# An attention and feed-forward kernel on one core: the first half of a weight loaded through another engine's queue, and a new order

## The chip, the cores and the metric

The kernel runs on one core of a Trainium2 chip. The metric is the device time of one execution in microseconds (us); lower is better. A core has five engines, each with its own instruction stream executed in order: PE (TensorE, matrix multiply; its weight loads are listed as PEld), DVE (VectorE), ACT (ScalarE), POOL (GpSimd) and SP (SyncE, which here only issues transfers). Transfers between the large memory and the core's own memory (DMAs) are issued by SP, ACT or POOL, each into a queue of its own, and are carried out by 16 DMA engines that all queues share.

## The reference

Inputs are q, k and v of 4 batches, 8 heads, 768 positions and 64 columns, a flag for each head, and three weights, all in float32.

```
scores = q @ k^T / 8
retrieval heads (flags 1 0 1 0 0 0 1 0): causal mask
the other heads: causal mask, and key among the first 4 or query - key < 64
a = softmax(scores);  attn = a @ v
x = attn, heads side by side: 3072 x 512
out = maximum(x @ w1, x @ w2) @ w_out      (512 -> 1024 -> 512)
```

## The kernel before, in words

The work is cut into eight halves: four batches (`b`), each in two halves of 384 queries (`hf`). Heads are taken in four pairs. Of (b, hf) = (0, 0), called half A, and (0, 1), called half B, the names appear in the list of first loads.

For a half, `prepare` casts q, k and v to bfloat16 (`cast`, `vcast`, on POOL, DVE or ACT), turns q and k on PE (`turn`, L756) and copies them out (`unturn`). `attend` computes scores (`S`, L945), exponentials on ACT (L964), masks on DVE (L983), weighted sums (`W`, L1008), and scales them into `x` (L1035). For batch 0, `x` is turned on PE (`TX`, L1128) and copied to `xt`.

The feed-forward part uses maximum(h1, h2) = relu(h1 - h2) + h2. So `prep_weights` makes w12 = w1 - w2 (`sub`, L1164, four quarters on DVE), casts w2 to bfloat16 (`w2b`), turns it on PE (`P`, L1180), copies it out (`w2t`) and multiplies it by w_out (`P2`, L1198) into `w2o`. `forward` then needs, for a half, eight up-projections of 4 matmuls with w12 (`F`, L1219), a relu each (L1243), and for each of three blocks of 128 rows 12 matmuls into one bank (L1269): 8 with w_out and 4 with `w2o`. Output is copied by `take_out` and stored at L1288.

**What sets the order.** No instruction is placed by hand. Each piece of work is an `Op` with a cost for each engine that may do it, the pieces that it depends on, and a rank. `Order.run` (L197) is a planner in Python that runs when the kernel is built: it keeps a clock, gives each engine as it comes free the ready piece of lowest rank, and emits the instructions in that order. Its times are guesses; on the chip each engine goes through its stream in the emitted order and waits on semaphores that follow from the data. The ranks (`RANK`, `FRONT`, `FRONT_STEP`, `STEP`, `FF_STEP`) and the margins are the result of a search. While PE has no ready work and the planner's clock is under 38 us (`WARM_UNTIL`), the planner puts in a matmul on a zero tile (`warmer`, L503).

**Loads.** `LOADS` (L405) lists the first loads: A and B are q and k of the two halves (L551, 768 KB each, rows of 768 bytes), Av and Bv their v in three pieces (L561, 256 KB each, rows of 256 bytes), w10, w11, w20, w21 the two halves of w1 and w2 (L637, 1 MB each, rows of 2 KB), wo0 to wo3 the quarters of w_out (L651, cast to bfloat16 on the way). All but w_out go through SP's queue. w_out goes through POOL's, and each quarter is first held back by a small copy (L650) that reads from an earlier load: which one follows from `PACE`: with 1 it is the last but one of the loads listed ahead of it (w_out itself not counted), with 2 the last but two. The staging memory has three slots: half A in the first, half B in the second, w2 in the third, and w1 in the first again, so w1 is loaded when half A's casts are done.

For queues the planner has a model: a load becomes active `DMA_LATE` after its issue, active queues share the rate by `grain` (its guess at a row's weight), and a queue takes no more loads when the `parts` of those in it exceed `RING`; SP then waits.

Of the kernel before, what the change touches and what calls it, by code (L numbers as in the profile page):

```python
# [15 lines left out]
ACT = mybir.ActivationFunctionType  # L16
# [98 lines left out]
class Op:  # L115
# [1 line left out]

    __slots__ = (
        "costs", "emit", "deps", "lat", "data", "end", "left", "users", "ready", "rank",
        "claims", "frees", "margin", "tag", "port", "bias", "share", "parts", "grain",  # L120
    )

    def __init__(self, costs, emit, deps=(), lat=0.13, data=None, rank=0.0, claims=(), frees=(),
                 margin=0.0, tag=None, port=(), bias=None, share=1.0, parts=1024, grain=18.0):
        self.costs, self.emit, self.lat, self.data, self.rank = costs, emit, lat, data, rank
        self.deps = [o for o in deps if o is not None]
        self.claims, self.frees, self.margin, self.tag = claims, frees, margin, tag
        self.port, self.bias, self.share, self.parts = port, bias or {}, share, parts
        self.grain = grain
        self.end, self.ready, self.users = None, 0.0, []  # L130


class Order:
# [63 lines left out]
    def run(self, names, allowed):  # L197
        free = dict.fromkeys(("PE", "ACT", "DVE", "POOL", "SP"), 0.0)
        free["SP"], free["PE"], free["POOL"] = 0.75, PE_BEGINS, MASKS_MADE - 0.45
        done_pe = []  # L200

        def used(t, span=3.4):
# [78 lines left out]
        while events:  # L281
            t = events[0][0]
            while events and events[0][0] <= t + 1e-9:
                _, _, o = heapq.heappop(events)
# [22 lines left out]
            while again:  # L307
# [22 lines left out]
                for relaxed in (False, True):  # L330
                    chosen = None
                    for n in ("S", *names) if last == "S" else names:
                        if at[n] >= len(self.lists.get(n, ())):
                            continue
                        o = self.lists[n][at[n]]
# [13 lines left out]
                    if chosen:  # L349
                        n, o = chosen  # L350
# [33 lines left out]
CAST_QK = {'POOL': 0.46, 'DVE': 0.27, 'ACT': 0.4}  # L384
CAST_V = {'POOL': 0.3, 'DVE': 0.26, 'ACT': 0.26}
RANK = {
    'cast': 1.75, 'vcast': 14.3, 'unturn': 1.4, 'mix_k': 0.0, 'mix_v': -21.35, 'exp': 1.0,
    'mask': -1.9, 'norm': -5.7, 'take_x': 2.25, 'turn': -5.95, 'w2b': 7.1, 'sub': -11.6, 'w2t':
    -11.15, 'wob': -4.75, 'w2o': -6.8, 'relu': -2.6, 'load': 7.35, 'out': -9.5, 'h2': 11.0,
    'table': -2.65, 'vload': 3.85,  # L390
}
NLD = 3
NQB = 4
# [43 lines left out]
ENTER_S = 0.1  # L437
# [7 lines left out]
FRONT = (  # L445
    {'mix_k': -29.1, 'mask': -2.4, 'unturn': -6.1, 'exp': -1.5, 'vcast': 3.3, 'cast': -24.7,
    'norm': -13.8}, {'vcast': 27.9, 'unturn': -12.7, 'exp': 5.4, 'mask': 33.1, 'norm': 9.1,
    'mix_k': 37.9, 'cast': -12.4},
)
FRONT_STEP = (30.1, 7.2)  # L450
UNTURN_BIAS = ({'ACT': 1.0}, {'ACT': 1.0})
SHARED = 0.89
UP_PARTS = 2


def tile_three_full_heads(
# [3 lines left out]
    nc = tc.nc  # L460
    B, H, S, D = q.shape
# [15 lines left out]
    w2b = keep.tile([128, KC, d_ff], BF16, name="w2b")  # L477
# [27 lines left out]
    order = Order(8, dummy, WARM_UNTIL)  # L505
    op, pe = order.op, order.pe
    eng = {"ACT": nc.scalar, "DVE": nc.vector, "POOL": nc.gpsimd}
    T = {}

    def copy(e, out, in_):  # L510
# [13 lines left out]
    def act(n):  # L524
        return 0.065 + n / 1200

    def dma(mb, emit, deps=(), rate=0.31, rank=0.0, old=None, parts=1024, grain=18.0):
        asked.append(rank)
        o = op({"SP": 0.5}, emit, deps, data=mb / rate, rank=rank + 1e-4 * len(asked), parts=parts, grain=grain)
        if old is not None:  # L530
            later.append((o, old))
        return o
# [11 lines left out]
    def load_half(b, hf, kinds=(0, 1, 2)):  # L544
# [11 lines left out]
            loads[b, hf, t].append(dma(mb, emit, old=old, rate=RATE["first"] if t == 0 and (b, hf) != (0, 0) else RATE["long"], grain=36.0))  # L556

        def piece(t, src, i):
            def emit(_):
                r0 = HALF * hf + 128 * i  # L560
                nc.sync.dma_start(  # L561
                    out=lds[:, s, t, :, i * D:i * D + D],
                    in_=src[b, :, r0:r0 + 128, :].rearrange("h p d -> p h d"),
                )
            loads[b, hf, t].append(dma(0.262, emit, old=old, rate=RATE["v"]))
# [62 lines left out]
    def load_up(name, src, c):  # L628

        if name not in T:  # L630
            s, staged_old[name], tenants[name] = slot()
            T[name] = lds[:, s].rearrange("p t h c -> p (t h c)")[:, 0:KC * d_ff] \
                .rearrange("p (c f) -> p c f", f=d_ff)
        n = d_ff // UP_PARTS

        def emit(_):
            nc.sync.dma_start(  # L637
                out=T[name][:, :, c * n:c * n + n],
                in_=src.rearrange("(c p) f -> p c f", p=128)[:, :, c * n:c * n + n],
            )  # L640
        return dma(
            2.097 / UP_PARTS, emit, old=staged_old[name], rate=RATE["w"] if UP_PARTS == 4 else RATE["w half"],
            parts=512, grain=180.0 / UP_PARTS,
        )

    def load_down(c, behind):

        def emit(_):
            for o in behind:
                nc.gpsimd.tensor_copy(out=landed, in_=place_of[o])  # L650
            nc.gpsimd.dma_start(  # L651
                out=wob[:, 2 * c:2 * c + 2],
                in_=wo.rearrange("(c p) f -> p c f", p=128)[:, 2 * c:2 * c + 2],
            )
# [1025 lines left out]
```

## Time and profile before

| | before |
|---|---|
| median of 3 runs (lowest to highest) | 182.91 us (182.77 to 182.97) |
| the profiled execution's own time | 183.0 us |
| its span, first to last instruction | 181.3 us |
| clock granted to TensorE | 0.998 |

The profiled execution has 1.7 us outside its span. A line of a timeline gives start and length in us, engine (a `q` behind it: its sequencer, which issues transfers and doesn't count as busy), line of the kernel, operation, output and inputs, and count; in brackets is how long the engine had been idle and what ended the wait. A line of the windows view gives a stretch, its length, the busy time and number of instructions of PE, PEld, DVE, ACT and POOL, TensorE's granted clock, the load of the DMA engines and the rate in GB/s. A line of issues ends with the KB of a transfer and the us from its issue to its landing. A line of a queue gives packets, MB and the share of the 16 engines.

### The profile page before, as it was taken

Reading aid. Unit: us, or ns where it says so; the run is one execution under the profiler, and the core shown is the slowest. Engines: PE = TensorE matmul, PEld = TensorE weight load, DVE = VectorE, ACT = ScalarE, POOL = GpSimd, SP = SyncE. Lnnn points to the kernel's source line nnn. Section 1 sums busy time; section 2 is a strip of 40 time slices with the busy share of each in tenths; the row PEclk is TensorE's granted clock in tenths of the full one; section 3 lists DMA queues with packets and bytes.
Section 4 is the critical chain, followed back from the end, with each engine's and each line's share of the span. In section 5 each row is a group of like instructions: output and inputs, shape, how many; then the busy total and the mean of one; then the engine's idle time right before and its main releaser. Section 6 shows DMA issues by size and latency. Waiting matters only on the chain.

```text
span 181.3 us, 4937 instructions
## 1 busy us (share of the span) xinstructions
PE 171.4 (95%) x1806; PEld 106.3 (59%) x1826; DVE 103.8 (57%) x301; ACT 130.9 (72%) x289; POOL 43.8 (24%) x88
## 2 busy tenths in 40 slices
PE   7999969999998999999999999999999999999992
PEld 7966836565655666556554764555466545545561
DVE  5688976798979997256666685944647500000000
ACT  3567965795999999999999895566798524525431
POOL 6524500100518049839665000000000000000000
PEclk9999999999999999999999999999999999999999
DMA  4999999999899999999999999930641052012013
GB/s 128 332 306 228 358 205 196 391 321 265 234 278 265 322 268 228 238 157 220 189 159 128 202 171 126 206 124 0 66 140 58 4 145 116 7 61 116 0 68 116
DMA packets 72529, 32.37 MB, mean 179 GB/s; under 512 B 53938, under 2 KB 67506, under 8 KB 72498
## 3 DMA queue, kind: packets, MB, share of 16 engines
q1 hardware_dynamic: 52448, 28.45, 64.8%
q0 software_dynamic: 19904, 3.41, 26.7%
q8 instruction: 16, 0.26, 0.6%
q10 hardware_dynamic: 146, 0.13, 0.2%
q14 instruction: 15, 0.12, 0.2%
HBM read 25.17 MB, written 6.29 MB: 174 GB/s over the span
## 4 chain that ended last, share of the span: by engine, by line
PE 66%; DMA 14%; DVE 6%; issue 4%; SPq 4%; POOL 1%; ACT 1%; DVEq 0%; POOLq 0%; ACTq 0%
PE ps L1269 32%; PE ps L1219 17%; PE ps L945 7%; PE ps L1008 5%; DMA ld<-in_k_dram 5%; DMA ld<-in_v_dram 5%; DMA wob<-in_moe_w_out_dram 5%; SPq L551 3%; PE ps L756 2%; DVE x L1035 2%; SPq L561 2%; PE ps L1198 1%; DVE at L983 1%; POOL qb L514 1%; ACT at L964 1%
## 5 line engine op out<-in xcount | busy, mean ns | idle before, releaser
L964 ACT ACTIVATE at<-ps 128x512 bf16<-128x512 f32 (+2 forms) x134 | 65.1, 577 | 10.0 <-PE ps L945 9.2
L1269 PE MATMUL ps<-wob,g 128*128 128x512 bf16 (+1 forms) x194 | 45.9, 370 | 0.5 <-issue 0.3
L1219 PE MATMUL ps<-xt,w 128*128 128x384 bf16 x256 | 45.9, 326 | 0.0
L1219 PEld LDWEIGHTS <-w 128*128 128x128 bf16 x256 | 23.7, 98 | 14.7
L983 DVE TENSOR_TENSOR at<-at,tab 128x1024 bf16<-128x1024 bf16 (+5 forms) x49 | 25.3, 529 | 10.0 <-ACT at L964 9.9
L1243 ACT ACTIVATE g<-ps 128x384 bf16<-128x384 f32 x51 | 25.2, 502 | 5.9 <-PE ps L1219 5.7
L1269 PEld LDWEIGHTS <-g 128*128 128x128 bf16 x200 | 18.2, 98 | 18.7 <-issue 0.2
L512 ACT COPY ot<-ps 128x512 f32<-128x512 f32 (+1 forms) x19 | 10.7, 566 | 20.6 <-PE ps L1269 20.5
L1269 PE MATMUL ps<-w2o,xt 128*128 128x512 bf16 (+1 forms) x91 | 24.3, 370 | 0.5
L1008 PEld LDWEIGHTS <-at 128*128 128x128 bf16 x477 | 19.6, 97 | 7.4 <-issue 0.8
L1035 DVE TENSOR_TENSOR x<-ps,rez 128x192 f32 x64 | 22.7, 355 | 1.5
L1008 PE MATMUL ps<-vb,at 128*128 128x65 bf16 x387 | 21.4, 193 | 0.2
L945 PE MATMUL ps<-qk 64*128 64x128 bf16 (+1 forms) x322 | 19.9, 230 | 0.3
L945 PEld LDWEIGHTS <-qk 64*128 64x128 bf16 x322 | 11.9, 94 | 10.4 <-issue 7.8
L514 POOL CAST qb<-ld 128x384 bf16 (+1 forms) x21 | 9.7, 494 | 27.1 <-DVE x L1035 12.3
L1269 PEld LDWEIGHTS <-xt 128*128 128x128 bf16 x100 | 9.2, 98 | 8.7
L503 PE MATMUL ps<-warmer 128*128 128x128 bf16 x137 | 12.7, 254 | 1.2 <-POOL warmer L1613 1.2
L756 PE MATMUL ps<-tab,qb 128*128 128x128 bf16 x144 | 12.0, 219 | 1.8 <-POOL qb L514 0.5
L512 ACT CAST qb<-ld 128x192 bf16 (+1 forms) x24 | 8.7, 412 | 5.2 <-DMA ld<-in_k_dram 2.1
L1025 DVE RECIPROCAL rez<-ps 128x6 f32<-128x6 f32 x32 | 5.2, 183 | 11.6 <-PE ps L1008 11.4
L503 PEld LDWEIGHTS <-warmer 128*128 128x128 bf16 x137 | 10.8, 117 | 1.4 <-POOL warmer L1613 1.2
L756 PEld LDWEIGHTS <-qb 128*128 128x128 bf16 x144 | 9.0, 98 | 4.1 <-POOL qb L514 1.1
(69 smaller groups left out, 168.7 us busy)
## 6 DMA issues: line engine op xcount, KB each, us to landing
out_dram<-ot SPq DMA_DIRECT2D x23, 256.0 KB, 3.2
ld<-in_q_dram SPq DMA_DIRECT2D x6, 768.0 KB, 7.4
ld<-in_k_dram SPq DMA_DIRECT2D x6, 768.0 KB, 7.6
ld<-in_v_dram SPq DMA_DIRECT2D x18, 256.0 KB, 8.2
ld<-in_moe_w_dram SPq DMA_DIRECT2D x4, 1024.0 KB, 8.3
wob<-in_moe_w_out_dram POOLq DMA_DIRECT2D x4, 256.0 KB, 9.2
ld<-in_q_dram POOLq DMA_DIRECT2D x8, 96.0 KB, 11.3
ld<-in_k_dram POOLq DMA_DIRECT2D x8, 96.0 KB, 10.9
```

What stands on the lines that cost most here:

```text
L503: nc.tensor.matmul(banks[e][:, 0:128], lhsT=warm, rhs=warm, start=True, stop=True)
L512: nc.scalar.copy(out=out, in_=in_)
L514: eng[e].tensor_copy(out=out, in_=in_)
L756: nc.tensor.transpose(to[:, i], qbs[:, T["qb", n, hf] % NQB, t, i].rearrange("p h d -> p (h d)"), ident)
L945: nc.tensor.matmul(to.rearrange("p (i c) -> p i c", c=128), lhsT=lhsT, rhs=q_of(n, i, m)[rows], start=bk not in under, stop=True, skip_gro ...
L964: nc.scalar.activation(out=at[:, bk, 0:w], in_=bank(("ps", b, hf, t), part=bk)[:, 0:w], func=ACT.Exp, scale=scale,)
L983: eng[e].tensor_tensor(out=at, in0=at, in1=tbl, op=ALU.mult)
L1008: nc.tensor.matmul(po[:, hh, i - NT * hf, :], lhsT=ats[:, T["at", b, hf, t] % NAT, bk, e * 128:(e + 1) * 128], rhs=rhs, start=first, stop= ...
L1035: nc.vector.tensor_tensor(out=xs[:, (2 * b + hf) % NX, :, bass.ds(heads[2 * p + hh], 1), :], in0=po[:, hh, :, 0:D].unsqueeze(2), in1=z[:, ...
L1219: nc.tensor.matmul(bank(key)[:, 0:HALF], lhsT=w[:, kc, fc * 128:(fc + 1) * 128], rhs=xts[:, (2 * b + hf) % NXT, :, kc, :], start=(kc == 0) ...
L1243: nc.scalar.activation(out=g, in_=ph, func=ACT.Relu)
L1269: nc.tensor.matmul(bank(key)[:, cols], lhsT=lhsT, rhs=(w2o if kind == "x" else wob)[:, c, cols], start=(e == 0), stop=(e == len(steps) - 1),)
```

## The change

The first half of w2 (`w20`) is issued by ACT and no longer by SP. In the planner it depends on a piece that ends at 11.0 us and has rank -9, so ACT takes it as the first thing after the planner's 11.0 us. The list of loads changes; so, with `PACE` 2, do the loads that hold back w_out: wo0, wo1 and wo2 wait for the first piece of Av (before: second piece, third, third), wo3 for the second piece (before: w20). SP's limit goes from 4224 to 3300 parts, which holds three loads of 1024; the planner's latency becomes shorter for a load that waited for its queue; the `grain` of w_out goes from 90 to 50 and a half weight counts 768 parts, not 512. All ranks, margins and steps have new values. The other new names (`V_QUEUES`, `queues` for v) are there but empty or unused.

```diff
@@ begin
+            idle[e] = free[e]
...
-                push(t + (DMA_FIRST if t < 1.0 else DMA_LATE[e]), (e, o))
+                o.late = DMA_FIRST if t < 1.0 else max(RING_LATE, DMA_LATE[e] - max(0.0, t - max(o.ready, idle[e])))
+                push(t + o.late, (e, o))
...
-LOADS = ('A', 'B', 'Av', 'wo0', 'w20', 'wo1', 'wo2', 'w10', 'wo3', 'w21', 'Bv', 'w11')
-BIAS = {'DVE': 0, 'ACT': 0}
+LOADS = ('A', 'B', 'Av', 'wo0', 'wo1', 'wo2', 'w20', 'wo3', 'w21', 'Bv', 'w10', 'w11')
+BIAS = {'DVE': 0, 'ACT': 2.5}
...
-PACE = 1
+PACE = 2
...
-RING = {'SP': 4224, 'POOL': 6200, 'ACT': 4224}
+RING_LATE = 1.0
+RING = {'SP': 3300, 'POOL': 6200, 'ACT': 4224}
...
-    'first': 0.33, 'long': 0.32, 'v': 0.235, 'w': 0.355, 'w half': 0.39, 'wo': 0.37, 'cast':
+    'first': 0.33, 'long': 0.32, 'v': 0.225, 'w': 0.35, 'w half': 0.385, 'wo': 0.34, 'cast':
...
-STEP = 3.0
-FF_STEP = -2.9
-S_AFTER = 3
+STEP = 3.9
+FF_STEP = -2.2
+S_AFTER = 0
...
-MARGIN = {'W': 1.2, 'S': 0.2, 'F': 0.1, 'TQ': 0}
-X_MARGIN = 2.5
+MARGIN = {'W': 1.2, 'S': 0.2, 'F': 2.0, 'TQ': 0.8}
+X_MARGIN = 0.4
...
+BY_ACT = {'w20': 11.0}
+V_QUEUES = ()
...
+        by_act = name[:2] + str(c) in BY_ACT
+
         def emit(_):
-            nc.sync.dma_start(
+            queues["ACT" if by_act else "SP"].dma_start(
                 out=T[name][:, :, c * n:c * n + n],
                 in_=src.rearrange("(c p) f -> p c f", p=128)[:, :, c * n:c * n + n],
             )
         return dma(
-            2.097 / UP_PARTS, emit, old=staged_old[name], rate=RATE["w"] if UP_PARTS == 4 else RATE["w half"],
-            parts=512, grain=180.0 / UP_PARTS,
+            2.097 / UP_PARTS, emit, [order.given(BY_ACT[name[:2] + str(c)])] if by_act else (),
+            old=staged_old[name], rate=RATE["w"] if UP_PARTS == 4 else RATE["w half"],
+            parts=1536 // UP_PARTS, grain=180.0 / UP_PARTS, rank=-9.0 if by_act else 0.0,
+            by="ACT" if by_act else "SP",
         )
...
-            {"POOL": 0.9}, emit, behind, data=2.097 / 4 / RATE["wo"], grain=90.0, rank=-9.0, tag=f"wo{c}", parts=256
+            {"POOL": 0.9}, emit, behind, data=2.097 / 4 / RATE["wo"], grain=50.0, rank=-9.0, tag=f"wo{c}", parts=256
```

The new values of `RANK`, `FRONT`, `FRONT_STEP` and `UNTURN_BIAS` are left out here: all entries differ, and they enter only the planner's choice of what goes first.

More of the change, by code (lines that the diff above doesn't have):

```diff
@@ L119 @@
         "costs", "emit", "deps", "lat", "data", "end", "left", "users", "ready", "rank",
-        "claims", "frees", "margin", "tag", "port", "bias", "share", "parts", "grain",
+        "claims", "frees", "margin", "tag", "port", "bias", "share", "parts", "grain", "late",
     )
@@ L128, in __init__ @@
         self.port, self.bias, self.share, self.parts = port, bias or {}, share, parts
-        self.grain = grain
+        self.grain, self.late = grain, 0.0
         self.end, self.ready, self.users = None, 0.0, []
@@ L199, in run @@
         free["SP"], free["PE"], free["POOL"] = 0.75, PE_BEGINS, MASKS_MADE - 0.45
+        idle = dict(free)
         done_pe = []
@@ L386 @@
 RANK = {
[L387 to L390, printed above, removed]
+    'cast': 2.7, 'vcast': 12.75, 'unturn': 5.55, 'mix_k': 3.0, 'mix_v': -18.6, 'exp': -8.75,
+    'mask': 4.2, 'norm': -3.5, 'take_x': 1.25, 'turn': -2.9, 'w2b': 14.85, 'sub': -8.6, 'w2t':
+    -11.45, 'wob': -9.75, 'w2o': -2.15, 'relu': -6.45, 'load': 10.6, 'out': -10.45, 'h2': 9.35,
+    'table': -1.45, 'vload': -4.5,
 }
@@ L442 @@
 SHARE = {'S': 0.45, 'W': 0.8}
-MARGIN = {'W': 1.2, 'S': 0.2, 'F': 0.1, 'TQ': 0}
-X_MARGIN = 2.5
+MARGIN = {'W': 1.2, 'S': 0.2, 'F': 2.0, 'TQ': 0.8}
+X_MARGIN = 0.4
 FRONT = (
-    {'mix_k': -29.1, 'mask': -2.4, 'unturn': -6.1, 'exp': -1.5, 'vcast': 3.3, 'cast': -24.7,
-    'norm': -13.8}, {'vcast': 27.9, 'unturn': -12.7, 'exp': 5.4, 'mask': 33.1, 'norm': 9.1,
-    'mix_k': 37.9, 'cast': -12.4},
-)
-FRONT_STEP = (30.1, 7.2)
-UNTURN_BIAS = ({'ACT': 1.0}, {'ACT': 1.0})
+    {'mix_k': -26.4, 'mask': 13.8, 'unturn': -23.8, 'exp': 21.4, 'vcast': 6.5, 'cast': -6.4,
+    'norm': -43.7}, {'vcast': 58.2, 'unturn': -26.7, 'exp': 18.4, 'mask': 11.8, 'norm': 25.8,
+    'mix_k': 40.7, 'cast': 6.4},
+)
+FRONT_STEP = (37.7, -3.3)
+UNTURN_BIAS = ({'ACT': 1.0}, {'ACT': 0.5})
 SHARED = 0.89
 UP_PARTS = 2
+BY_ACT = {'w20': 11.0}
+V_QUEUES = ()
 def tile_three_full_heads(
@@ L507, in tile_three_full_heads @@
     eng = {"ACT": nc.scalar, "DVE": nc.vector, "POOL": nc.gpsimd}
+    queues = {"SP": nc.sync, "ACT": nc.scalar, "POOL": nc.gpsimd}
     T = {}
@@ L525, in act, with dma @@
         return 0.065 + n / 1200
-    def dma(mb, emit, deps=(), rate=0.31, rank=0.0, old=None, parts=1024, grain=18.0):
+    def dma(mb, emit, deps=(), rate=0.31, rank=0.0, old=None, parts=1024, grain=18.0, by="SP"):
         asked.append(rank)
-        o = op({"SP": 0.5}, emit, deps, data=mb / rate, rank=rank + 1e-4 * len(asked), parts=parts, grain=grain)
+        o = op(
+            {by: {"SP": 0.5, "ACT": 0.4, "POOL": 0.9}[by]}, emit, deps, data=mb / rate, rank=rank + 1e-4 * len(asked),
+            parts=parts, grain=grain,
+        )
         if old is not None:
@@ L558, in piece @@
         def piece(t, src, i):
+            by = next((e for *at, e in V_QUEUES if t == 2 and at == [b, hf]), "SP")
             def emit(_):
                 r0 = HALF * hf + 128 * i
-                nc.sync.dma_start(
+                queues[by].dma_start(
                     out=lds[:, s, t, :, i * D:i * D + D],
@@ L564, in emit @@
                 )
-            loads[b, hf, t].append(dma(0.262, emit, old=old, rate=RATE["v"]))
+            loads[b, hf, t].append(dma(
+                0.262, emit, old=old, rate=RATE["v"], rank=0.0 if by == "SP" else RANK["vload"], by=by,
+            ))
         long = (b, hf) in LONG
```

1 line of the change is left out of this document (removed).

## The prediction

> **What bounds the kernel now.** I read the page first: its span, its busy line and its groups.
>
> ```profile
> span 181.3 us, 4937 instructions
> PE 171.4 (95%) x1806; PEld 106.3 (59%) x1826; DVE 103.8 (57%) x301; ACT 130.9 (72%) x289; POOL 43.8 (24%) x88
> ...
> L503 PE MATMUL ps<-warmer 128*128 128x128 bf16 x137 | 12.7, 254 | 1.2 <-POOL warmer L1613 1.2
> ```
>
> PE is busy for 171.4 of 181.3 us, but 12.7 us of that are matmuls on the zero tile `warmer`, the fillers that the planner puts in while PE has nothing to do. So some 158.7 us are real work, which the change leaves alone, and the time is that work plus the stretches in which PE fills or waits. The windows view says where these are.
>
> ```profile
> 16.00:25.10 9.10, 7.31 (x131) 5.32 (x128) 8.39 (x27) 7.66 (x20) 3.71 (x8) 1.00 1.04 296
> 25.10:38.60 13.50, 13.31 (x169) 8.56 (x173) 9.54 (x21) 9.35 (x21) 0.63 (x2) 1.00 1.09 290
> ...
> 46.20:70.00 23.80, 22.96 (x294) 15.09 (x298) 21.36 (x60) 23.27 (x50) 10.49 (x25) 1.00 1.09 281
> ...
> 46.20:178.00 131.80, 129.34 (x1271) 76.17 (x1285) 66.96 (x195) 99.15 (x215) 31.45 (x53) 1.00 0.91 150
> ```
>
> The columns are the length, then the busy time of PE, PEld, DVE, ACT and POOL. PE lacks 9.10 - 7.31 = 1.8 us before 25.1 and next to nothing from there on; over the 131.8 us to 178 it lacks 2.5 us. So the front alone has something to give. PE's timeline shows how the front ends:
>
> ```profile
> 17.86 1.29 PE L1008 MATMUL ps<-vb,at 128*128 128x65 bf16 x32
> ...
> 25.12 1.47 PE L1198 MATMUL ps<-wob,w2t 128*128 128x512 bf16 x5 [1.66 <-DMA wob<-in_moe_w_out_dram]
> 26.43 0.67 PE L503 MATMUL ps<-warmer 128*128 128x128 bf16 x9
> ...
> 27.79 0.62 PE L1128 MATMUL ps<-tab,x 128*128 128x128 bf16 x8
> ...
> 38.03 2.76 PE L1219 MATMUL ps<-xt,w 128*128 128x384 bf16 x16
> ```
>
> At 25.12 PE had waited 1.66 us for the first quarter of w_out, without which the product w2 by w_out (L1198, `P2` in the planner) can't begin. At 38.03 the up-projection (L1219, `F`) begins, which needs w1. By then nearly all that PE can do without w1 is done. From 38 on work is plentiful: F and the output matmuls fill whatever attention leaves. **The end moves, to a first approximation, as the start of F at 38.03 moves.** Three things must come together for it: w1 landed, its difference with w2 made (L1164, on DVE), and PE's earlier work done. Here is the transfer side, SP's timeline and five of its landings:
>
> ```profile
> 3.65 2.19 SPq L551 DMA_DIRECT2D ld<-in_k_dram  x1
> 5.89 6.95 SPq L561 DMA_DIRECT2D ld<-in_v_dram  x3
> 12.88 2.96 SPq L637 DMA_DIRECT2D ld<-in_moe_w_dram  x2
> 15.88 10.88 SPq L561 DMA_DIRECT2D ld<-in_v_dram  x3
> 27.01 3.27 SPq L637 DMA_DIRECT2D ld<-in_moe_w_dram  x1
> ```
>
> ```profile
> ld<-in_k_dram SPq DMA_DIRECT2D x1, 768.0 KB, 9.6
> ...
> ld<-in_v_dram SPq DMA_DIRECT2D x1, 256.0 KB, 8.5
> ...
> ld<-in_v_dram SPq DMA_DIRECT2D x1, 256.0 KB, 6.7
> ...
> wob<-in_moe_w_out_dram POOLq DMA_DIRECT2D x1, 256.0 KB, 8.3
> ...
> ld<-in_moe_w_dram SPq DMA_DIRECT2D x1, 1024.0 KB, 8.3
> ```
>
> The order on SP is q, k of half A, q, k of half B, v of A in three pieces, both halves of w2, v of B, both halves of w1. Issues of 2.2 and 2.3 us each (B's k, each piece of v) are SP waiting for room in its queue. The landings are those of B's k (issued at 3.65, landed at 13.2), of the first piece of A's v (5.89, 14.4) and its last (after two issues of 2.3 us, at 10.6; 17.3), of the first quarter of w_out (16.76, 25.1, on POOL's queue) and of the first half of w1 (27.01, 35.3).
>
> **The change part by part.** *Both halves of w2 leave SP in one piece of 2.96 us; the first goes to ACT.* What ACT pays for one issue:
>
> ```profile
> 0.92 0.52 ACTq L1528 DMA_DIRECT2D raw<-in_is_retrieval_dram  x1
> ...
> 10.84 0.35 ACT L512 CAST qb<-ld 128x192 bf16 x1 [1.38 <-PE ps L945]
> ...
> 17.46 1.62 ACT L512 CAST vb<-ld 128x192 bf16 x6 [1.11 <-DMA ld<-in_v_dram]
> ```
>
> ```profile
> L637 SPq DMA_DIRECT2D ld<-in_moe_w_dram x4: 612/1612/3267, 12.9 to 30.3; - x4
> ```
>
> ACT's only issue so far takes 0.52 us for 64 bytes; an unhindered half of w2 on SP takes 0.61; a hindered one takes 2.96 - 0.61 = 2.35. ACT's queue is empty at 11 us, so I take 0.6, with 0 and 2.35 as ends. Behind it on ACT stand the exps and casts of half A. They end with a wait for v (1.11 us at 17.46), which covers 0.6; if that wait went, 0.6 us would reach PE's weighted sums (L1008).
>
> *What flows when.* The queues' packet counts for three stretches, 13.5 to 15 (v alone), 17.2 to 18.2 (w2 alone) and 25.2 to 29.2 (B's v beside w_out), and the bytes around 16:
>
> ```profile
> q1 hardware_dynamic: 1284, 0.32, 127.8%
> ```
>
> ```profile
> q1 hardware_dynamic: 192, 0.39, 104.7%
> ```
>
> ```profile
> q0 software_dynamic: 562, 0.54, 79.0%
> q1 hardware_dynamic: 1147, 0.29, 42.8%
> ```
>
> ```profile
> 16.00:17.00 1.00, 0.95 (x14) 0.45 (x12) 0.97 (x3) 0.35 (x1) 0.36 (x2) 1.00 0.50 126
> 17.00:18.00 1.00, 0.94 (x14) 0.46 (x13) 0.49 (x2) 0.54 (x3) 0.91 (x3) 1.00 1.00 373
> ```
>
> A's v is 3 x 1024 packets of 256 B; alone they go at 1284 / 1.5 = 856 per us, so 3.6 us in all. Half of w2 is 512 packets of 2 KB; alone 192 per us, so 2.7 us. Together that is 6.3 us. Before, the two took from 13.2 (B's k landed) to 20.2:
>
> ```profile
> 16.64 0.18 POOL L650 COPY landed<-ld 1x1 f32<-1x1 f32 x1 [2.35 <-DMA ld<-in_v_dram]
> 16.76 0.92 POOL L651 DMA_DIRECT2D wob<-in_moe_w_out_dram  x1
> ...
> 20.20 0.17 POOL L650 COPY landed<-ld 1x1 f32<-1x1 f32 x1 [0.65 <-DMA ld<-in_moe_w_dram]
> ```
>
> which is 7.0 us. The 0.7 us between is the hole at 16 to 17 (126 GB/s and then 373): v was through, w2 not yet begun, because SP had been held on its issue. With w2 in a queue of its own the hole is filled: **w1 can land 0.7 us sooner**, at 34.6. If packets alternate, w2 takes 512 x (1/192 + 1/856) = 3.3 us and lands near 17 in place of 20.2, and v of A is pushed from 17.3 to about 19.8 or later.
>
> *w_out.* Its first three quarters now wait for the first piece of v (before: second, third and third), and the fourth for the second piece in place of w2. v's first piece landed at 14.4; beside w2 it lands between 15 and 17.1. So the first issue stays near 16.7. But it then flows beside 256 B packets for a while: the stretch from 25.2 shows 562 packets of w_out in 4 us there, 1.8 us for a quarter's 256. With 2 us until a transfer moves (w2's first issue ended at 15.2, its packets ran at 17), it lands at 20.5 at best, at 25.1 as before at worst. I take 22. P2 then starts some 3 us earlier and fills the 1.66 us of waiting. The fillers between 16.3 and 38 can go too, though they stand in the order by the planner's guess:
>
> ```profile
> L503 PE MATMUL ps<-warmer x35: 218/219/219, 19.0 to 26.9; 128*128 128x128 bf16 x35
> ```
>
> They follow one another at (0.67 - 0.22) / 8 = 0.056 us (the nine at 26.43), so 35 make 2.0 us.
>
> *F's start.* DVE's and PE's rows:
>
> ```profile
> 18.81 0.33 DVE L514 CAST vb<-ld 128x192 bf16 x1
> ...
> 29.66 0.41 DVE L514 COPY xt<-ps 128x512 bf16<-128x512 bf16 x1
> ...
> 36.32 2.35 DVE L1164 TENSOR_TENSOR w<-ld 128x1024 bf16<-128x1024 f32 x2
> ```
>
> The first difference began 1.0 us after w1 landed, since DVE was at other work, and takes half of 2.35. With w1 at 34.6 and DVE at once free F could start at 34.6 + 1.2 + 0.2 = 36.0, 2.0 us sooner. PE has 1.8 + 0.2 + 2.0 = 4.0 us of waiting and fillers to give for it, so w1 is the tighter bound. I take half of 2.0, because DVE's queue in front of the differences is ordered by ranks that the trace can't show.
>
> *The rest.* All ranks, margins, rates and steps are new, so every engine's order is. The limit of three loads on SP changes only what the planner believes: on the chip SP waits for room either way. From 46.2 on ACT is busy 23.27 of 23.80 us, PE 22.96; the order there decides 2.5 us of waiting. Nothing in the trace says whether the new order waits more. Ends: 1 us less, 2.5 more; I take 0, nearest to the row.
>
> **Sum.** 183.0 (the profiled execution, 1.7 around its span) - 1.0 = 182.0; the median of the runs is 182.91, 0.1 below the profiled one, so **181.9**.
>
> **The rivals.** *More of the same:* F at 36.0 and a little less waiting behind: 182.9 - 2.0 = 180.9. For it: 4.0 us of slack on PE. Against: DVE is busy 8.39 of 9.10 us up to 25.1. Chance 0.12.
>
> *The same bytes, another order:* v, w2, w_out, w1 must all land before F, and if the hole only moves, F stays at 38.03: 182.9. For it: 290 and 296 GB/s in both windows before F; SP's lost 2.35 us gave way to a single hole. Chance 0.12. The Trainium skill, DMA: Bandwidth & Descriptors, section Issuing engines are not separate DMA queues, speaks for this one: issuing from several engines, it says, saves only the sequencer's time, as all share the same DMA engines. By it the gain would be nothing; this trace has no second large load on ACT's queue to test it, though it has the hole.
>
> *v of A starved (slower):* after w2 three quarters of w_out compete with A's v. In the stretch from 25.2 the small packets fell to 1147 / 4 = 287 per us beside w_out, a third of 856. Of v's 3072 packets some 2560 are left at 17, 1450 gone by 18.7, the other 1100 at 287 per us take 3.9 us: v at 22.6 or later in place of 17.3. The slot for w1 frees when v's casts end (19.1 now; w1 is issued at 27.01, so 7.9 us of cover), and x turned at 27.79 to 29.66 has 8.4 us before F. Both hold. But W of half A is PE's work before 25, by the groups from 17.5 to 25:
>
> ```profile
> L1008 PE MATMUL ps<-vb,at 128*128 128x65 bf16 x48 | 2.5, 193 | 0.1
> ```
>
> 48 matmuls at 1.29 / 32 = 0.04 each (the row at 17.86) are 1.9 us of PE's queue; if it goes behind 23 and w_out still lands at 25, nothing takes its place, PE has no slack from 25.1 to 38.6, and F starts 1.9 us later: 184.8. It decides once w_out's first quarter lands later than about 24. Chance 0.20.
>
> *The later order is worse:* 2.5 us more waiting behind 46.2, less the 1.0 won: 184.4. ACT's full stretch from 46 to 70 speaks for it, PE's plentiful work against. Chance 0.14.
>
> **How the numbers follow.** The forecast, gains of 0.4 to 1.6 us, has 0.42. Two thousandths of the time (0.37 us) are about what a measurement of this kernel can tell from none, so faster is 0.42 + 0.12 = 0.54, the same 0.12, slower 0.20 + 0.14 = 0.34. The range takes in both slower cases and the full gain: 180.8 to 184.9; the forecast's own is 181.3 to 182.5.
>
> **What would show it.** Right: w2's first half lands near 17, no hole of 126 GB/s around 16, P2 begins at 22 or so, fewer than 35 fillers after 16.3, F begins near 37, and the waiting after 46 is still near 2.5 us. Wrong: A's v casts after 23 with PE on fillers meanwhile; F at 38 or later although w1 landed sooner; ACT's issue over 1 us; or more than 3.5 us of PE's waiting after 46, which would make the new order, not the queue, the cause.

## The result and the profile after

The change makes the kernel slower: median 184.77 us of 7 runs (183.87 to 186.39) against 182.77 us of 7 runs of the kernel before; the ratio is 1.0106 [1.0066, 1.0146]. I had forecast 181.9. An execution with a mean granted clock of 0.991 takes longer than its like: of the kernel before, 6 of 34 in the last comparison took 183.8 to 184.3 us, against a median of 182.6 for the others; the ratios hold both kinds (here the 186.39 is one). The profiled execution took 184.77 us. The page of the kernel after, the same three lines as before:

```profile
span 183.2 us, 4978 instructions
PE 173.1 (95%) x1830; PEld 106.6 (58%) x1830; DVE 105.1 (57%) x322; ACT 126.2 (69%) x268; POOL 42.8 (23%) x88
...
L509 PE MATMUL ps<-warmer 128*128 128x128 bf16 x141 | 12.9, 250 | 1.2 <-POOL warmer L1631 1.2
```

The span grew by 1.9 us. PE's busy time grew by 1.7, but this trace also holds 24 more matmul records than that of before; a second profile of the same kernel (`after_again`, 1809 records) has 171.1 us, so that sum tells little. The page alone doesn't say where the time went. The windows view does (stretch, length, busy time of PE, PEld, DVE, ACT and POOL, granted clock, DMA share, GB/s):

```profile
16.00:25.10 9.10, 6.46 (x112) 5.13 (x109) 5.87 (x17) 4.68 (x11) 3.21 (x9) 1.00 1.14 283
25.10:38.60 13.50, 12.48 (x144) 7.35 (x141) 9.30 (x27) 10.22 (x23) 0.75 (x2) 1.00 1.02 279
...
46.20:178.00 131.80, 130.91 (x1299) 76.50 (x1298) 71.42 (x224) 95.04 (x197) 30.75 (x52) 1.00 0.87 148
```

Up to 25.1 PE now lacks 2.64 us (1.8 before), to 38.6 another 1.02 (0.19 before), but behind 46.2 only 0.9 (2.5 before). The front lost. The last figure is a weak one: more work was left for that stretch, 28 more records stand in it, and `after_again` lacks 2.05 there. What came back behind the front is read better from the start of the up-projection. PE's timeline shows for what it waited:

```profile
20.89 0.62 PE L1198 MATMUL ps<-tab,w2b 128*128 128x128 bf16 x8 [1.43 <-ACT w2b L519]
...
23.70 0.40 PE L1026 MATMUL ps<-vb,at 128*128 128x65 bf16 x8 [1.19 <-ACT vb L519]
...
27.61 1.03 PE L1216 MATMUL ps<-wob,w2t 128*128 128x512 bf16 x4
...
29.64 1.22 PE L1198 MATMUL ps<-tab,w2b 128*128 128x128 bf16 x16 [1.00 <-DVE w2b L521]
...
40.99 5.65 PE L1237 MATMUL ps<-xt,w 128*128 128x384 bf16 x32
```

The weighted sums of half A (L1026) begin at 23.70, in place of 17.86, behind 1.19 us of waiting for v. The product with w_out (L1216) begins at 27.61, in place of 25.12. The second half of w2 brings a third wait. The up-projection begins at 40.99, in place of 38.03: 2.96 us later. The span minus that start is 142.2 us, before 143.3, so 1.1 us came back behind it; 2.96 - 1.1 is the 1.9 that the span grew. ACT's and SP's timelines give the loads:

```profile
10.81 0.42 ACTq L653 DMA_DIRECT2D ld<-in_moe_w_dram  x1
...
19.79 1.04 ACT L519 CAST w2b<-ld 128x1024 bf16<-128x1024 f32 x1 [2.45 <-DMA ld<-in_moe_w_dram]
...
23.30 1.11 ACT L519 CAST vb<-ld 128x192 bf16 x4 [1.48 <-DMA ld<-in_v_dram]
```

```profile
12.88 2.20 SPq L653 DMA_DIRECT2D ld<-in_moe_w_dram  x1
15.12 13.40 SPq L573 DMA_DIRECT2D ld<-in_v_dram  x3
28.78 2.10 SPq L653 DMA_DIRECT2D ld<-in_moe_w_dram  x2
```

w2's first half, issued by ACT at 10.81, is in at 19.8 (20.2 before). The last of A's v is in at 23.3 (17.4 before). SP stands on B's v from 15.12 to 28.5, so that w1 is issued at 28.78, in place of 27.01. Two landings and two stretches show the rest:

```profile
wob<-in_moe_w_out_dram POOLq DMA_DIRECT2D x1, 256.0 KB, 9.5
...
ld<-in_moe_w_dram SPq DMA_DIRECT2D x1, 1024.0 KB, 6.6
```

```profile
16.00:17.00 1.00, 0.98 (x15) 0.77 (x13) 1.00 (x4) 1.00 (x3) 1.00 (x3) 1.00 1.04 376
31.00:32.00 1.00, 1.00 (x7) 0.41 (x6) 1.00 (x3) 0.91 (x1) 0.40 (x2) 1.00 0.72 80
```

The first quarter of w_out (issued at 14.54) is in at 24.0, 1.1 us sooner than before. w1's first half (issued at 28.78) is in at 35.4, as before (35.3). The hole at 16 to 17 is filled, 376 GB/s for 126, and another has opened at 31, 80 GB/s, where SP had been held. And the packets from 16 to 17, by queue (q10 is ACT's, q1 SP's):

```profile
q10 hardware_dynamic: 183, 0.37, 103.1%
q1 hardware_dynamic: 5, 0.00, 0.6%
```

In that microsecond w2 moves at nearly the rate that it has alone (192), and A's v stands still.

The sizes and times of the packets in the trace tell the rest (v's have 256 bytes, w2's 2 KB). w2's first half began to move at 14.4, and v's third piece, which before began at 14.6, began at 16.9. Of that piece's 1024 packets 960 were through by 18.5; before, by 16.1. The last 64, a sixteenth, took until 22.8, more than half of them at one in each 0.10 us beside w_out; before they were through at 17.0, and with w_out's old release (`a_late` below) at 19.8. Each load ends with 16 packets of 4 bytes: 15 of v's came by 18.6, the last at 22.7. So w2 moved v back by some 2.4 us, and the rest of its lateness is that of one share in 16.

### The profile page after: what moved, and what is told of

It is laid out like the page before. It is cut to its first block, busy times and chain, and to the rows that moved or that the text cites. A ratio compares the mean times of both kernels' runs of the same rounds, so it can differ in the third digit from the quotient of the medians.

```text
span 183.2 us, 4978 instructions
## 1 busy us (share of the span) xinstructions
PE 173.1 (95%) x1830; PEld 106.6 (58%) x1830; DVE 105.1 (57%) x322; ACT 126.2 (69%) x268; POOL 42.8 (23%) x88
## 3 DMA queue, kind: packets, MB, share of 16 engines
q0 software_dynamic: 19904, 3.41, 24.2%
## 4 chain that ended last, share of the span: by engine, by line
PE 71%; DMA 9%; DVE 8%; SPq 6%; ACT 2%; issue 2%; DVEq 0%; ACTq 0%
PE ps L1287 32%; PE ps L1237 21%; DMA ld<-in_moe_w_dram 9%; PE ps L963 6%; PE ps L1026 6%; SPq L573 4%; SPq L561 3%; PE ps L1216 2%; PE ps L774 2%; DVE w L1182 2%; DVE at L1001 1%; ACT at L982 1%; DVE vx L521 1%; DVE qb L521 1%; PE ps L1146 1%
## 5 line engine op out<-in xcount | busy, mean ns | idle before, releaser
L982 ACT ACTIVATE at<-ps 128x512 bf16<-128x512 f32 (+2 forms) x134 | 64.4, 583 | 5.7 <-PE ps L963 5.3
L1287 PE MATMUL ps<-wob,g 128*128 128x512 bf16 (+1 forms) x200 | 47.2, 371 | 0.0
L1261 ACT ACTIVATE g<-ps 128x384 bf16<-128x384 f32 x55 | 27.0, 494 | 9.1 <-PE ps L1237 8.5
L519 ACT COPY ot<-ps 128x512 f32<-128x512 f32 (+1 forms) x22 | 12.8, 580 | 25.7 <-PE ps L1287 25.7
L1001 DVE TENSOR_TENSOR at<-at,tab 128x1024 bf16<-128x1024 bf16 (+5 forms) x49 | 24.5, 512 | 7.6 <-ACT at L982 7.1
L1026 PEld LDWEIGHTS <-at 128*128 128x128 bf16 x477 | 19.4, 97 | 8.1 <-issue 1.7
L1053 DVE TENSOR_TENSOR x<-ps,rez 128x192 f32 x64 | 22.8, 356 | 1.6
L1026 PE MATMUL ps<-vb,at 128*128 128x65 bf16 x387 | 20.4, 193 | 1.2 <-ACT vb L519 1.2
L963 PEld LDWEIGHTS <-qk 64*128 64x128 bf16 x322 | 12.2, 94 | 9.6 <-issue 7.3
L521 DVE CAST qb<-ld 128x384 bf16 (+1 forms) x38 | 12.3, 378 | 1.4 <-DMA ld<-in_q_dram 0.9
L521 POOL CAST vb<-ld 128x192 bf16 x28 | 9.6, 387 | 14.2 <-DMA ld<-in_v_dram 14.2
L519 ACT COPY qk<-ps 128x768 bf16<-128x768 bf16 x14 | 11.6, 840 | 0.4 <-PE ps L774 0.2
L509 PEld LDWEIGHTS <-warmer 128*128 128x128 bf16 x141 | 10.8, 115 | 1.6 <-POOL warmer L1631 1.2
L521 POOL CAST qb<-ld 128x384 bf16 (+1 forms) x11 | 4.9, 471 | 27.8 <-DVE x L1053 14.2
```

The source lines that it names most:

```text
L509: nc.tensor.matmul(banks[e][:, 0:128], lhsT=warm, rhs=warm, start=True, stop=True)
L519: nc.scalar.copy(out=out, in_=in_)
L521: eng[e].tensor_copy(out=out, in_=in_)
L963: nc.tensor.matmul(to.rearrange("p (i c) -> p i c", c=128), lhsT=lhsT, rhs=q_of(n, i, m)[rows], start=bk not in under, stop=True, skip_gro ...
L982: nc.scalar.activation(out=at[:, bk, 0:w], in_=bank(("ps", b, hf, t), part=bk)[:, 0:w], func=ACT.Exp, scale=scale,)
L1001: eng[e].tensor_tensor(out=at, in0=at, in1=tbl, op=ALU.mult)
```

## The experiments

My theory after this reading: the loss comes from w2's first megabyte getting ahead of the third piece of A's v. Rivals: the second queue as such; w_out's early release; the new order of the engines. "Early" below is the new release of w_out, "late" the old one. All kernels compute the whole reference. F is the start of the up-projection, and "v in" is the landing of v's last piece where the trace names it, else the first cast, or the copy, that follows it. Each ratio is taken against executions of the kernel before made beside it (medians 182.4 to 182.96 us). "v in", F and span are those of one profiled execution, which took between 0.9 us less and 0.7 us more than the median, in `c_mix` 1.5 us less.

| kernel | order | w2's first half | w_out | v in | F | span | median us, ratio [95%] |
|---|---|---|---|---|---|---|---|
| before | old | SP, behind v | late | 17.4 | 38.03 | 181.3 | 1 |
| after | new | ACT at 10.8 | early | 23.3 | 40.99 | 183.2 | 184.77, 1.0106 [1.0066, 1.0146] |
| after_again | new | ACT at 10.8 | early | 23.2 | 40.71 | 183.4 | 185.05, 1.0103 [1.0062, 1.0143] |
| a_sp_mid | new | SP, ahead of v's last piece | early | 21.8 | 39.21 | 181.3 | 183.78, 1.0037 [1.0001, 1.0073] |
| a_sp | new | SP, behind v | early | 17.2 | 38.76 | 180.6 | 182.84, 0.9998 [0.9970, 1.0027] |
| a_late | new | ACT at 11.0 | late | 20.7 | 39.85 | 182.2 | 183.96, 1.0068 [1.0038, 1.0099] |
| a_late_again | new | ACT at 10.9 | late | 20.7 | 39.87 | 182.0 | 183.87, 1.0060 [1.0034, 1.0086] |
| a_act13_late | new | ACT at 11.7 | late | 20.6 | 39.88 | 182.1 | 183.81, 1.0078 [1.0056, 1.0100] |
| a_sp_late | new | SP, behind v | late | 17.5 | 38.92 | 180.9 | 182.51, 0.9982 [0.9945, 1.0019] |
| a_first_late | new | ACT at 4.8 | late | - | 42.53 | 184.7 | 186.5 (one run) |
| a_replan | new, planned without ACT | SP, behind v | early | 17.4 | 37.81 | 180.7 | 183.16, 1.0015 [0.9984, 1.0047] |
| b_act | old | ACT at 10.9 | late | 20.7 | 40.82 | 184.0 | 185.49, 1.0143 [1.0090, 1.0196] |
| b_act13 | old | ACT at 11.9 | late | 21.0 | 41.09 | 184.2 | 185.42, 1.0154 [1.0124, 1.0184] |
| b_act145 | old | ACT at 14.1 | late | 17.4 | 39.14 | 182.3 | 183.29, 1.0005 [0.9968, 1.0042] |
| b_sp_front | old | SP, ahead of all of v | late | 20.0 | 40.40 | 182.8 | 184.58, 1.0148 [1.0092, 1.0204] |
| b_early | old | SP, behind v | early | 17.4 | 47.82 | 189.7 | 191.54, 1.0475 [1.0410, 1.0539] |
| b_early2 | old | SP, behind v | early, last quarter free | 17.4 | 37.32 | 181.4 | 182.78, 0.9982 [0.9951, 1.0012] |
| c_mix | old loads, new steps and ranks | SP, behind v | late | 17.4 | 37.94 | 181.4 | 184.6, 1.0080 [1.0044, 1.0116] |

### The change taken apart: a_sp, a_late, a_sp_late

In `a_sp` SP issues w2's first half right behind A's v, all else as after; `a_late` keeps ACT's queue and gives w_out its old release; `a_sp_late` does both.

```diff
@@ a_sp: load of A's v, after its last piece
+                if (b, hf, t, i) == (0, 0, 2, NT - 1):
+                    behind_v.pop()()
@@ a_sp: load of w2's first half
-        def emit(_):
-            queues["ACT" if by_act else "SP"].dma_start(
+        def issue():
+            nc.sync.dma_start(
...
+        def emit(_):
+            if by_act:
+                behind_v.append(issue)
@@ a_late: release of w_out (quarters behind v's second, third and third piece and w2's first half)
-            for o in behind:
+            for o in HOLD[c]():
+    HOLD = [lambda: [loads[0, 0, 2][1]], lambda: [loads[0, 0, 2][2]], lambda: [loads[0, 0, 2][2]], lambda: [w2_in[0]]]
```

> The new order on every engine but one thing: w2's first half goes out on SP again, behind the third piece of A's v, as before. w_out stays released early. If w2 on ACT's queue is what starves A's v (it landed at 23.3 in the changed kernel, 17.4 before), v lands near 18 and the time falls from 184.8 to about 183. If w_out's early release does it, v still lands after 21 and the time stays at 184 to 185. If the new order itself is at fault, v lands early and the time still stays at 184 to 185.

> The new order, w2 on ACT, but the copies that hold back the quarters of w_out read what they read before (second, third, third piece of A's v, first half of w2). Starved by w2's queue: v still after 21, 184 to 185. Starved by w_out: v at 19 to 20 (only pushed by w2), 183 or so. Order at fault: 184 to 185 whatever v does.

> The new order with both transfers as before: w2 on SP behind A's v, w_out held back as before. If the transfers are the cause, landings are those of before and the time is 182 to 183. If the order is the cause, landings are those of before and the time stays at 184 or more.

With w2 back on SP the loss is gone, whichever release w_out has (0.9998 and 0.9982); with ACT it stays at two thirds without the early release (1.0068; v at 20.7 and 183.96 us lie between the two cases that I had expected). So w2's place makes most of the loss. w_out's early release adds to it beside w2, as far as the runs tell, and nothing clear without it. In `a_sp` DVE, PE and the long stretch read:

```profile
37.49 2.34 DVE L1191 TENSOR_TENSOR w<-ld 128x1024 bf16<-128x1024 f32 x2
```

```profile
38.76 5.65 PE L1246 MATMUL ps<-xt,w 128*128 128x384 bf16 x32
```

```profile
46.20:178.00 131.80, 129.32 (x1270) 76.52 (x1285) 69.28 (x217) 94.78 (x197) 30.82 (x52) 1.00 0.87 150
```

The order of each engine is that of the kernel after, so the two can be set side by side. F starts 2.23 us sooner than after, and so does w1's first difference (L1191, at 37.49). The kernel after has on DVE:

```profile
36.69 0.69 DVE L521 CAST w2o<-ps 128x512 bf16<-128x512 f32 x1 [1.47 <-PE ps L1216]
...
39.72 2.35 DVE L1182 TENSOR_TENSOR w<-ld 128x1024 bf16<-128x1024 f32 x2
```

The difference comes 4.3 us after w1 landed. Ahead of it on DVE stands the cast of `w2o`, which had waited 1.47 us for PE's product with w_out, and that product stands on PE behind the late sums of half A and the late second half of w2. So F's start follows PE's front and not w1's landing. `a_late` says the same from the other end: there w1 lands 1.2 us sooner than before (34.1), and F still starts at 39.85.

```profile
39.85 3.37 PE L1238 MATMUL ps<-xt,w 128*128 128x384 bf16 x18
```

### The old order with w2 elsewhere: b_act, b_sp_front

Only the place of w2's first half is changed in the kernel before. `b_act`: ACT issues it ahead of its first exponential. `b_sp_front`: SP issues it ahead of all of A's v, without a second queue.

```diff
@@ b_act: first exponential of half A
+            if (b, hf, t, bk) == (0, 0, 0, 0):
+                by_act.pop()(nc.scalar)
             nc.scalar.activation(
@@ b_sp_front: load of A's v, first piece
+                if (b, hf, t, i) == (0, 0, 2, 0):
+                    by_act.pop()(nc.sync)
```

> The old order on every engine, with one thing moved: w2's first half is issued by ACT ahead of its first exponential (about 11 us). If w2's queue is the cause, v lands after 20 and the time rises from 182.8 to 184 or more. If only the order or w_out's release is, it stays within 0.4 of 182.8.

> The old order, w2's first half on SP's queue but ahead of A's v: the byte order of the change without a second queue. w2 lands near 16.5, v near 20. If the loss comes from v standing behind 1 MB of w2, the time is 184.5 to 185.5, like the old order with w2 on ACT (185.5). If the second queue adds to it (stragglers, w2 at 19.8 and v past 21), the time is 183 to 184.

The rows of v's sums and F, `b_act` and then `b_sp_front`:

```profile
21.13 1.46 PE L1018 MATMUL ps<-vb,at 128*128 128x65 bf16 x32 [3.04 <-DVE vb L514]
...
40.82 2.76 PE L1229 MATMUL ps<-xt,w 128*128 128x384 bf16 x16
```

```profile
20.39 1.95 PE L1018 MATMUL ps<-vb,at 128*128 128x65 bf16 x32 [2.56 <-DVE vb L514]
...
40.40 2.76 PE L1229 MATMUL ps<-xt,w 128*128 128x384 bf16 x16
```

Both lose alike, 1.0143 and 1.0148 (four runs each). The loss in the old order needs neither a second queue nor the new order: it is enough that w2 goes ahead of v. PE waits 3.0 and 2.6 us for v and then runs at half the clock for a while (last section); F starts 2.8 and 2.4 us later than before.

### When ACT issues: b_act13, a_act13_late, b_act145, a_first_late

The same issue at other places of ACT's stream: behind the exponential of piece 1 (`b_act13`, `a_act13_late`, meant for about 13.4 us), behind one of piece 2 (`b_act145`), and ahead of all planned work (`a_first_late`). The two with the new order have w_out's old release.

```diff
@@ b_act13 and a_act13_late: behind an exponential; b_act145 has (0, 0, 2, 0)
+            if (b, hf, t, bk) == (0, 0, 1, 1):
+                by_act.pop()(nc.scalar)
@@ a_first_late
+    on_act.pop()(nc.scalar)
     order.run(PE_LISTS, lambda name, o: True)
```

> The old order, w2's first half issued by ACT behind its fourth exponential, at about 13.4 us, when SP has just issued the last piece of A's v (12.8). Turns by issue (what was issued first flows first, whichever queue): v lands at 17.4 as before, w2 right behind it without the hole, near 19.5, and the time is 182.0 to 183. Turns by queue (ACT's queue takes the DMA engines from SP's while it has packets): v lands at 19 to 21 and the time is 183.5 to 185.

> The new order with w_out held back as before, and w2's first half issued by ACT at about 13.4 us. Turns by issue: landings of the run with w2 on SP or a little better, 181.5 to 182.7, which would beat both kernels. Turns by queue: 183.5 to 184.5, like the run with w2 on ACT at 11.

> The old order, w2's first half issued by ACT behind the first exponential that waits for half A's third group of scores (about 14.5 us), so that SP's issue of A's v (over at 12.8 to 13.1) is certainly done; in the run that aimed at 13.4 ACT issued at 11.9, inside SP's last issue. If it is the place in issue that counts, v lands at 17.4 again, W begins near 17.9 and F near 38, 182 to 183. If ACT's queue takes the engines whenever it has packets, v lands past 19 and the time is 184 or more.

> The new order, w_out held back as before, w2's first half issued by ACT as soon as it has the head order (about 5 us), while SP's queue holds q and k with rows of 768 bytes. For the packet counts of the two queues. Turns by issue: w2 flows after B's k, in one block, near 13 to 16. Turns by queue: it flows from 7 or so, SP's packets fall to nearly nothing for 2.7 us, and B's q and k land 2.7 us later. Packets in turn, one of each: w2 takes 512 x (1/192 + 1/425) = 3.9 us with 768 byte packets beside it. The time is 185 or more by all three.

The first two missed their time: the issue came at 11.9 and 11.7, ahead of the exponentials in front of it in the stream, so they only repeat `b_act` (1.0154) and `a_late` (1.0078). In `b_act145` it came at 14.14, after SP's issue of v's last piece was over (13.3):

```profile
14.14 0.41 ACTq L638 DMA_DIRECT2D ld<-in_moe_w_dram  x1
...
17.45 1.61 ACT L512 CAST vb<-ld 128x192 bf16 x6 [0.67 <-DMA ld<-in_v_dram]
```

A's v is in at 17.4, as before, and the loss is gone: 1.0005 [0.9968, 1.0042]. F, which I had expected near 38, stands at 39.14 in the profiled execution: SP was held on B's v until 27.8 and w1 landed at 36.1. ACT's queue as such costs nothing beyond that interval, and it gains nothing. That agrees with the half of the rule that the prediction cites from the Trainium skill (DMA: Bandwidth & Descriptors, section Issuing engines are not separate DMA queues): several issuing engines save only the sequencer's time. `b_act` shows the half that the rule doesn't tell: another engine's issue can also pass a load whose own issue is still held (v at 20.7 in place of 17.4).

`a_first_late` puts w2 beside k and q, whose rows have 768 bytes. Its queues from 10 to 12 us:

```profile
q10 hardware_dynamic: 265, 0.54, 75.1%
q1 hardware_dynamic: 266, 0.19, 31.7%
```

Packet for packet, one of 2 KB for one of 768 bytes: w2 takes three quarters of the engines, and everything that attention starts with comes late (F at 42.53, 186.5 us in one run against 182.4).

### Byte order or queue: after_again, a_late_again, a_sp_mid

One comparison for the sizes: the kernel after, `a_late`, and the kernel after with `queues[...]` replaced by SP, so that the planner's own place for w2 falls between v's second and third piece.

```diff
@@ a_sp_mid (after_again and a_late_again are after and a_late)
-            queues["ACT" if by_act else "SP"].dma_start(
+            nc.sync.dma_start(
```

> The changed kernel itself, on the same chip as the next three, to compare with. 184.3 to 185.0 where before gives 182.4 to 183.0; F near 41.

> The changed kernel with w_out held back as before. If the early release adds to the loss while w2 goes through ACT (F was at 39.9 without it, 41.0 with it), 0.6 to 1.2 us under the changed kernel on the same chip. If the two runs differed by chip only, within 0.3 of it.

> The changed kernel with w2's first half on SP's queue between the second and the third piece of A's v, which is the order in which the bytes moved in the changed kernel, and no second queue. If the byte order is the loss, w2 lands near 17.5, the third piece of v at 20 or later, and the time is within 0.5 of the changed kernel's. If the second queue is, v and w2 land earlier than there (23.3, 19.8) and the time is 182.5 to 183.5.

SP's issue of w2, ACT's casts of v and PE's F in `a_sp_mid`:

```profile
11.04 2.19 SPq L653 DMA_DIRECT2D ld<-in_moe_w_dram  x1
```

```profile
21.78 1.11 ACT L519 CAST vb<-ld 128x192 bf16 x4 [0.24 <-DMA ld<-in_v_dram]
```

```profile
39.21 5.65 PE L1237 MATMUL ps<-xt,w 128*128 128x384 bf16 x32
```

The order of the bytes alone, on one queue and beside the early w_out, pushes v from 17.2 (`a_sp`) to 21.8 and makes 1.0037 [1.0001, 1.0073]. With ACT's queue in addition v comes at 23.2, w2's second half at 28.6 in place of 27.1, and the ratio is 1.0103 [1.0062, 1.0143]: 1.27 us more by the medians, 1.2 by the ratios, with intervals that overlap by a little. So neither of the two outcomes that I had expected came: the byte order makes part of the loss here. The early release adds the step from 1.0060 to 1.0103, about 0.4%; the two intervals overlap, but the result itself (1.0106) against `a_late` (1.0068) points the same way.

### The rest of the change: a_replan, c_mix, b_early, b_early2

`a_replan` has the new settings with no load on ACT, so the planner makes its own order for that. `c_mix` has the loads of before with the new steps, margins, bias and general ranks. `b_early` and `b_early2` have the old order with w_out's early release.

```diff
@@ a_replan
-BY_ACT = {'w20': 11.0}
+BY_ACT = {}
@@ c_mix
-STEP = 3.0
-FF_STEP = -2.9
-S_AFTER = 3
+STEP = 3.9
+FF_STEP = -2.2
+S_AFTER = 0
...
@@ b_early2: three quarters behind v's first piece, the last behind nothing (b_early: the last behind v's second piece)
+    HOLD = [lambda: [loads[0, 0, 2][0]]] * 3 + [lambda: []]
```

> The changed kernel without its entry for ACT: w2's first half goes through SP and the planner makes its order for that, with the new ranks, list of loads and limits. If the queue was the loss and the rest is sound, 181.5 to 182.7, at or under the run that kept the order and moved the load back (182.5 to 182.8). If the ranks only suit a w2 that comes early, 183.5 or more.

> The old kernel's loads, queues, weights' ranks and first two halves (its front ranks kept by taking the difference out of the general ones), with the new steps, margins, ACT's bias and general ranks for everything behind. The new order had 1.2 us less behind F's start (141.9 to 142.3 against 143.2) and 0.8 more before it. If the two parts add up: F near 38, span less F near 142, 181.6. If the gain behind F was only the slack that a late F leaves, span less F is 143 and the time that of before.

> The old order and queues, w_out released as in the changed kernel (three quarters behind the first piece of A's v, the fourth behind the second). Alone it should do little: v lands by 17.5 before w_out's packets flow, w2's second half is slowed by 1 to 2 us. 182.6 to 183.4; over 184 if the early release were a cause by itself.

> The old order and queues, three quarters of w_out released behind the first piece of A's v and the fourth right behind them with no copy of its own; in the run before, that copy read memory into which w1 had been issued and waited 17.7 us for it. Now 182.5 to 183.5, w_out's quarters landing between 22 and 30, if the early release does little by itself; 184 or more if it is a cause alone.

`a_replan` has v in at 17.4, F at 37.81 and 1.0015 [0.9984, 1.0047]: the planner's own order without ACT's load is no better and no worse than before. `c_mix` was a miss: I had hoped that the 1.1 us won behind F come with the steps and ranks, but its span minus F is 181.4 - 37.94 = 143.5 us (before 143.3), and the runs are slower, 1.0080. The profiled execution is the fastest of its ten, so its trace doesn't show where that loss lies. The gain is not just what a late F leaves, for `b_act` has F at 40.82 and 143.2 us behind it. It goes with the new order as a whole (`a_sp`: 180.6 - 38.76 = 141.8), and I can't name one setting for it.

`b_early` was a miss of another kind. The copy that holds back the last quarter read memory that w1 is loaded into next:

```profile
34.88 0.17 POOL L650 COPY landed<-ld 1x1 f32<-1x1 f32 x1 [17.67 <-DMA ld<-in_moe_w_dram]
```

```profile
40.93 4.40 PE L1199 MATMUL ps<-wob,w2t 128*128 128x512 bf16 x10 [7.96 <-DMA wob<-in_moe_w_out_dram]
```

POOL waited 17.67 us for w1, PE 7.96 us for the quarter. It says nothing of the early release. `b_early2` does, without that copy:

```profile
37.32 2.76 PE L1220 MATMUL ps<-xt,w 128*128 128x384 bf16 x16
...
46.66 1.51 PE L757 MATMUL ps<-tab,qb 128*128 128x128 bf16 x24 [1.67 <-POOL qb L514]
```

w_out's first quarter is in at 22.6, near my 22, and F starts 0.7 us sooner. It is given back at 46.66, where PE waits 1.67 us for POOL's cast of q: 0.9982 [0.9951, 1.0012]. No version beats the kernel before by more than its interval.

## Why the prediction was wrong

The step that failed is **What flows when**, and **F's start** with it. Point by point:

- *"Half of w2 lands near 17 in place of 20.2, and v of A is pushed to about 19.8 or later."* The landing was 19.8, so w2 won 0.4 us and not 3 (15 of its 16 closing packets came by 17.7, the last at 19.1). v was not slowed by turns, as I took it: its third piece began only at 16.9, when most of w2 was through, and the last sixteenth of it then met w_out: 23.3. The words "or later" were left without a price in the forecast.
- *"w1 can land 0.7 us sooner, at 34.6."* It landed at 35.4. The hole at 16 was filled as I said, but SP then stood on B's v until 28.5, and a new hole opened at 31. What the rival "the same bytes, another order" said of holes held. The sum behind the 0.7 us was also off: it counts from 13.2, but v's first packets moved at 12.2.
- *"w_out's first quarter at 22, P2 starts some 3 us earlier."* It landed at 24.0, inside the stated ends, and P2 started at 27.61, later than before, because PE stood on the waits for w2 and v first. With v in place it landed at 22.6 in the old order (`b_early2`), but at 24.2 and 24.0 in `a_sp` and `a_replan`.
- *"w1 is the tighter bound" for F.* Not here: in the kernel after the difference waited 4.3 us after w1's landing for DVE, which waited for PE's product; in `a_late` w1 was in sooner and F was still late. The 35 fillers that should have gone became 47.
- *ACT's issue, 0.6 us.* It took 0.42 us. Right, and it had nothing to do with the loss.
- *"The rest", taken as 0.* It measured -1.1 us of span behind F, and -0.6 in `after_again`, about my lower end of -1. The waiting after 46.2, which I had named as its sign, doesn't show it: `a_sp` wins 1.4 us behind F with 2.5 us of that waiting, as before. The new order is sound; it gives 0.6 to 1.4 us back behind F, and in `a_sp` costs 0.7 us ahead of it.
- *The rival "v of A starved"* described what happened, with its place: v at 22.6 or later (23.3), w_out at the point of decision of about 24 (24.0), PE without other work, fillers in its place. Its 184.8 us beside the measured 184.77 is partly luck: it had F 1.9 us later and nothing behind it; measured were 2.96 later and 1.1 back. Its 22.6 for v is luck too: it had 2560 of v's packets left at 17, by turns that didn't take place, and 1100 of them slowed by w_out. The trace has some 1020 left at 17, and only the last 64 were slowed.

Left open: why v's third piece stood still. It fits that w2 was issued at 10.8, while SP was still held on issuing that piece (until 12.83), and that nothing happened when ACT issued after it (`b_act145`); how the queues take up waiting loads no run shows. Nor does any run show why one share in 16 lags, as it did before the change too (17.0 against 16.1). Open too is why the second queue costs 1.27 us more than the same place on SP (`a_sp_mid`); v's last share came through at 21.3 there, against 22.6 in `after_again`.

## What to carry to other kernels

A second issuing queue brought no more bytes per second here (283 and 279 GB/s in the two stretches before F, against 296 and 290); what it changed is who went first. Before a load is moved to an idle queue, look at which load the first queue is still held on at that moment, and at what the critical engine does if that load comes as late as the whole of the new one. Ask also what else will be moving by then: the last sixteenth of v was in at 19.8 without w_out beside it and at 22.8 with it. And a fixed order passes such a delay on: whatever stands behind the late operand on PE, and then on DVE behind PE, is late with it, even if its own data landed on time.

## What the runs showed of the hardware

- TensorE's clock fell at waits shorter than I had thought. In `b_sp_front` PE waited 2.56 us, up to 20.39, and the clock from 20 to 22 was 0.50:

```profile
18.00:20.00 2.00, 0.00 (x0) 0.00 (x0) 0.01 (x1) 0.01 (x1) 0.79 (x2) 1.00 0.88 174
20.00:22.00 2.00, 1.61 (x30) 1.61 (x30) 1.77 (x9) 2.00 (x8) 1.87 (x5) 0.50 0.98 361
```

  The half clock lasted 3.4 us (20.0 to 23.4; in `b_act` 22.05 to 25.46). In `a_first_late` it fell at 18.2, 1.4 us into a wait of 2.42 us (one of 1.14 us stood some 4 us earlier), while a whole wait of 1.77 us in `a_sp_late` left it at 1.00; so the length of one wait doesn't decide it alone. The Trainium skill (TensorE: Matmul & The Clock Gate, Part 1: The HAM clock gate) says that the clock falls after at least one idle window of about 3.4 us; here it fell at shorter waits.
- Where two loads moved side by side, the queues took turns by packets and not by bytes: 265 of 2 KB to 266 of 768 bytes in `a_first_late`, 0.54 MB to 0.19. The small rows lose. They don't always take turns: in the kernel after it was 183 to 5 from 16 to 17.
- A load's landing can hang on its last sixteenth: 960 of 1024 packets through by 18.5 and the last 64 by 22.8 in the kernel after, 16.1 and 17.0 before.
- ACT's issue of a transfer ran ahead of the activations in front of it: in `b_act13` it came at 11.86, while the exponential that stands ahead of it ended at 13.6, so "in order" holds for what ACT computes and not for its issues:

```profile
11.28 1.08 ACT L972 ACTIVATE at<-ps 128x512 bf16<-128x512 f32 x2
11.86 0.41 ACTq L638 DMA_DIRECT2D ld<-in_moe_w_dram  x1
12.25 0.35 ACT L512 CAST qb<-ld 128x192 bf16 x1
12.49 1.10 ACT L972 ACTIVATE at<-ps 128x512 bf16<-128x512 f32 x2
```
